# Turning the second half of q of batch 0 on VectorE, with the keys laid over row groups, in a fused attention and feed-forward kernel

## The chip, the cores and the metric

One core of one Trainium2 chip. The metric is device time in microseconds (us) of one execution.

## The reference, cut to what matters

```python
# batch 8, heads 8, seq 1024, head_dim 64, k_proj 64
k_proj = einsum('ks,bhsd->bhkd', E, k);  v_proj = einsum('ks,bhsd->bhkd', F, v)
attn   = softmax(q @ k_proj^T / 8)                   # 64 keys for each query
x      = (attn @ v_proj), heads side by side         # 8192 x 512
h      = max(x @ w1, x @ w2, x @ w3)                 # 512 -> 768
out    = h @ w_out                                   # 768 -> 512
```

## The kernel before: the parts concerned

The matmuls of the scores take q with the head dimension on the partitions (`qT`). For later batches VectorE turns q (`q_flip`, 0.69 us for each 128x512), and the kernel reads the result as 32x32 blocks, each turned in its place; the scores run as 32-row matmuls on eight tiles of the array (L141: 32 of 256 columns take 0.59 us from the first start to the next L208, though each is 0.27 us long). The second half of q of batch 0 is turned by TensorE in the kernel before:

```python
def q_up0():
    for g in range(NPAIR):
        for sl in range(4):
            for u in range(2):                      # 32 matmuls against the identity
                nc.tensor.matmul(out=ps[u*D:(u+1)*D, 4+g, sl*P:(sl+1)*P],
                                 lhsT=q_1[:, HEAD[2*g+u], sl, :], rhs=ident, start=True, stop=True)
    for j in range(2):                              # two casts out of PSUM, one on each engine
        (nc.vector.tensor_copy if j else nc.scalar.copy)(out=qT[0][...], in_=ps[...])

def scores_up0():
    for g, bank in ((0, 4), (1, 5), (2, 6), (3, 7)):
        scores0(1, g, bank)                         # 2 matmuls of 64 rows x 512 columns
    for g in (0, 2):
        nc.scalar.activation(out=pT[0][:, g:g+2, 1, :], in_=ps[:, 4+g:6+g, :], func=AF.Exp, scale=scale)
```

Loads go out from GpSimd in one order: k and v of batch 0, w1, w2, first half of w3, **second half of q of batch 0**, **second half of w3**, w_out, then k, v and q of batch 1. `kv(b)` projects keys and values of batch b, and sends the keys through a transposing DMA (`kpT`); `scores(b, u)` waits for that DMA. What each batch does is placed by slots; a slot is one 128x512 product of the feed-forward (four or six matmuls). In the first 18 us TensorE also runs `warmup` matmuls on zeros while it waits for loads. `sums` adds up the denominators of the softmax, and AV is the product of the attention weights with the projected values. `ps` is the tile in PSUM that every matmul writes: eight banks of 512 columns.

```python
if b == 0:
    at(9, scores_up0); at(12, sums0, 1, 4); at(19, kv, 1)
    # q_flip(1, g) at 21, 22, 24, 25; load_behind_turn(2) at 22
    at(27, scores, 1, 0); at(30, scores, 1, 1); at(33, sums, 1)
    # ... cut
elif b == 1:
    at(2, kv, 2)
    # ... cut
    at(9, load_behind_turn, 3, "kvq"); at(8, scores, 2, 0); at(12, scores, 2, 1)
    at(15, av1, 1); at(15, sums, 2); at(15, log, 1); at(16, recip, 0); at(18, recip, 1)
```

The softmax here doesn't subtract the row's maximum and nothing guards it: scores larger than these inputs give would overflow.

## Time and profile before

| | before |
|---|---|
| median of the first 3 runs | 396.2 us (395.97 to 396.36) |
| span of the profiled run | 394.4 us |
| TensorE busy | 98% |
| TensorE waits between 45 and 92 us of the span | 0.7 us for the turned keys of batch 2 |

The lines of the profile are in the prediction.

### The profile page before, as it was taken

Reading aid. Unit: us, or ns where it says so; the run is one execution under the profiler, and the core shown is the slowest. Engines: PE = TensorE matmul, PEld = TensorE weight load, DVE = VectorE, ACT = ScalarE, POOL = GpSimd, SP = SyncE. Lnnn points to the kernel's source line nnn. Section 1 sums busy time; section 2 is a strip of 40 time slices with the busy share of each in tenths; the row PEclk is TensorE's granted clock in tenths of the full one; section 3 lists DMA queues with packets and bytes.
Section 4 is the critical chain, followed back from the end, with each engine's and each line's share of the span. In section 5 each row is a group of like instructions: output and inputs, shape, how many; then the busy total and the mean of one; then the engine's idle time right before and its main releaser. Section 6 shows DMA issues by size and latency. Waiting matters only on the chain.

```text
span 394.4 us, 6594 instructions
## 1 busy us (share of the span) xinstructions
PE 384.6 (98%) x2691; PEld 173.5 (44%) x2742; DVE 201.0 (51%) x296; ACT 162.5 (41%) x247; POOL 66.5 (17%) x109
## 2 busy tenths in 40 slices
PE   8999999999999999999999999999999999999996
PEld 4444444444444444444444444444444444444443
DVE  3347475655653476435763357525664456443342
ACT  4414447364326622455224732266234552222221
POOL 7442141062003401050000500000010000000000
PEclk9999999999999999999999999999999999999999
DMA  8999979979953995169611892121011111101023
GB/s 223 206 209 206 206 182 199 224 118 205 206 144 83 186 206 183 26 122 202 173 53 28 166 207 108 55 74 61 2 53 55 53 56 53 56 39 67 2 106 106
DMA packets 41437, 48.39 MB, mean 123 GB/s; under 512 B 9152, under 2 KB 36544, under 8 KB 41408
## 3 DMA queue, kind: packets, MB, share of 16 engines
q0 software_dynamic: 31776, 43.52, 53.2%
q1 hardware_dynamic: 8656, 3.41, 5.0%
q10 hardware_dynamic: 976, 1.05, 0.8%
q8 instruction: 21, 0.34, 0.3%
q14 instruction: 8, 0.07, 0.1%
HBM read 57.15 MB, written 16.78 MB: 187 GB/s over the span
## 4 chain that ended last, share of the span: by engine, by line
PE 91%; DMA 6%; issue 1%; POOL 0%; ACT 0%; DVE 0%; POOLq 0%
PE ps L208 58%; PE ps L233 19%; PE ps L119 3%; PE ps L155 3%; PE ps L431 3%; DMA w_sb<-in_moe_w_dram 2%; PE ps L141 2%; DMA k_t<-in_k_dram 2%; DMA kpT<-kp 1%; PE ps L246 1%; PE ps L422 1%; PE ps L226 1%; PE ps L264 0%; PE ps L311 0%; POOL k_t L347 0%
## 5 line engine op out<-in xcount | busy, mean ns | idle before, releaser
L208 PE MATMUL ps<-xT,w_sb 128*128 128x512 bf16 x1049 | 242.9, 379 | 1.7
L208 PEld LDWEIGHTS <-w_sb 128*128 128x128 bf16 x1080 | 103.6, 98 | 130.0 <-issue 8.6
L213 DVE TENSOR_TENSOR m<-ps,h1s 128x512 f32<-128x512 f32 x90 | 62.2, 691 | 132.4 <-PE ps L208 99.1
L233 PE MATMUL ps<-wo_sb,hT 128*128 128x512 bf16 x335 | 82.3, 379 | 0.5 <-issue 0.2
L211 ACT COPY h1s<-ps 128x512 f32<-128x512 f32 x90 | 53.0, 589 | 67.4 <-PE ps L208 67.0
L235 ACT COPY o_acc<-ps 128x512 f32<-128x512 f32 x58 | 34.0, 587 | 101.3 <-PE ps L233 85.8
L215 DVE TENSOR_TENSOR hT<-ps,m 128x512 bf16<-128x512 f32 x90 | 62.0, 689 | 10.2 <-PE ps L208 2.4
L240 POOL DMA_DIRECT2D out_dram<-o_acc x28 | 15.2, 543 | 263.2 <-ACT o_acc L235 261.1
L233 PEld LDWEIGHTS <-hT 128*128 128x128 bf16 x348 | 33.5, 98 | 41.4 <-issue 1.9
L173 DVE TENSOR_TENSOR xT<-ps,rinv 128x1024 bf16<-128x1024 f32 x28 | 33.5, 1218 | 8.8 <-PE ps L155 6.8
L146 ACT ACTIVATE pT<-ps 128x1024 bf16<-128x1024 f32 x28 | 27.1, 1021 | 7.3 <-PE ps L141 7.0
L101 DVE STREAM_TRANSPOSE qT<-q_t 128x512 f32<-128x512 f32 x28 | 18.6, 689 | 0.0
L87 POOL DMA_DIRECT2D v_t<-in_v_dram x21 | 15.3, 747 | 10.8 <-PE ps L208 4.2
L164 ACT ACTIVATE lns<-ps 128x1024 f32<-128x1024 f32 x14 | 13.6, 1021 | 5.8 <-PE ps L155 5.8
L167 ACT ACTIVATE rinv<-lns 128x1024 f32<-128x1024 f32 x14 | 14.7, 1062 | 0.0
L119 PE MATMUL ps<-k_t,eT 128*64 128x512 bf16 x56 | 13.4, 382 | 0.0
L121 PE MATMUL ps<-v_t,fT 128*64 128x512 bf16 x56 | 13.4, 381 | 0.0
L125 ACT CAST kp<-ps 64x512 bf16<-64x512 f32 x7 | 4.1, 579 | 18.5 <-PE ps L121 18.5
L87 POOL DMA_DIRECT2D k_t<-in_k_dram x14 | 10.6, 770 | 2.4 <-ACT o_acc L469 1.1
L87 POOL DMA_DIRECT2D q_t<-in_q_dram x14 | 10.6, 773 | 2.1 <-DMA wo_sb<-in_moe_w_out_dram 1.1
L431 PE MATMUL ps<-xT,w_sb 128*128 128x512 bf16 x46 | 10.6, 379 | 0.2 <-issue 0.2
L127 DVE COPY kp<-kp 64x1536 bf16<-64x1536 bf16 x7 | 3.9, 552 | 12.4 <-ACT kp L125 12.4
(84 smaller groups left out, 163.3 us busy)
## 6 DMA issues: line engine op xcount, KB each, us to landing
out_dram<-o_acc POOLq DMA_DIRECT2D x30, 512.0 KB, 3.1
q_t<-in_q_dram POOLq DMA_DIRECT2D x15, 512.0 KB, 12.1
k_t<-in_k_dram POOLq DMA_DIRECT2D x14, 512.0 KB, 12.6
v_t<-in_v_dram POOLq DMA_DIRECT2D x18, 256.0 KB, 14.8
v_t<-in_v_dram POOLq DMA_DIRECT2D x7, 512.0 KB, 14.8
w_sb<-in_moe_w_dram POOLq DMA_DIRECT2D x4, 384.0 KB, 10.1
k_t<-in_k_dram POOLq DMA_DIRECT2D x4, 256.0 KB, 8.0
w_sb<-in_moe_w_dram POOLq DMA_DIRECT2D x4, 192.0 KB, 9.6
```

The lines of the kernel that those rows point to most:

```text
L87: nc.gpsimd.dma_start(out=dst[b % NB][:, slots], in_=sv[:, heads])
L101: nc.vector.transpose(out=qT[b % NB][:, hs].bitcast(FP32).rearrange("p h n -> p (h n)"), in_=q_t[b % NB][:, hs].rearrange("p h si d -> p ( ...
L119: nc.tensor.matmul(out=ps[0:KP, bank, :], lhsT=eT[:, si, :], rhs=k_t[i][:, :, si, :], start=(si == 0), stop=(si == SI - 1))
L146: nc.scalar.activation(out=pT[i][:, 2 * u + gg].rearrange("p ch (t r n) -> p r (ch t) n", t=4, r=4), in_=ps[:, AB:AB + 4, gg * 256:(gg + 1 ...
L173: nc.vector.tensor_tensor(out=xT[b % 2][:, f::2, ch, :], in0=ps[:, bank:bank + 2, :], in1=rinv[ch].rearrange("p (u n) -> p u n", u=2), op= ...
L208: nc.tensor.matmul(out=ps[:, bank, :], lhsT=w_sb[i][:, ct, jt * P:(jt + 1) * P], rhs=xT[b % 2][:, ct, ch, :], start=(ct == 0), stop=(ct == ...
L211: nc.scalar.copy(out=h1s[jt % 2], in_=ps[:, bank, :])
L213: nc.vector.tensor_tensor(out=m12[jt % 2], in0=ps[:, bank, :], in1=h1s[jt % 2], op=ALU.max)
L215: nc.vector.tensor_tensor(out=hT[c % 2][:, jt, :], in0=ps[:, bank, :], in1=m12[jt % 2], op=ALU.max)
L233: nc.tensor.matmul(out=ps[:, bank, :], lhsT=hT[c % 2][:, jt, tt * P:(tt + 1) * P], rhs=wo_sb[:, jt, :], start=(jt == 0), stop=(jt == NJT - 1))
L235: nc.scalar.copy(out=o[:, tt, :], in_=ps[:, bank, :])
L431: nc.tensor.matmul(out=ps[:, bank, :], lhsT=w_sb[i][:, ct, jt * P:(jt + 1) * P], rhs=xT[0][:, ct, 0, :], start=(ct == 0), stop=(ct == NCT ...
```

## The change

The intent: spare TensorE 32 transposes. VectorE turns this half of q in one instruction (128x1024). The changed kernel reads its result as 32x32 blocks too, each turned in its place. With such blocks the scores run on 32-row groups, and the keys of batch 0 lie on all four of them; four matmuls with a selecting matrix do that early on, in the place of two warming matmuls. Besides, AV and sums of batch 2 move one slot.

```diff
+    def kp_up0():
+        for u in range(2):
+            for f in range(2):
+                nc.tensor.matmul(out=ps[:, u, f*256:(f+1)*256], lhsT=sel[:, 2*u+f, :], rhs=kpT[0][:, 0:NPAIR, 0, :], ...)
+            nc.vector.tensor_copy(out=kp_0[:, u]..., in_=ps[:, u, :])
     def q_up0():
-        # 32 matmuls, two casts
+        nc.vector.transpose(out=qT_1 as fp32, in_=q_1 as fp32)        # 128x1024
     def scores_up0():
-        # 8 matmuls of 64 rows x 512 columns, two exps
+        # for g, f, r, u: 64 matmuls of 32 rows x 128 columns on 4 row groups x 2 column groups
+        # four exps
@@ start
+    # sel: four VectorE copies from the identity
-    warmup(1, 2)
+    kp_up0()
     sums_part0(1)
-    warmup(4, 2)
+    warmup(3, 2)
@@ b == 1
-            at(8, scores, 2, 0)
+            at(9, scores, 2, 0)
-            at(15, av1, 1)  # and sums, log at 15, recip at 16 and 18
+            at(16, av1, 1)  # and sums, log at 16, recip at 17 and 19
```

More of the change, by code (lines that the diff above doesn't have):

```diff
@@ L40 @@
     warm = T([P, 512], BF16, "warm")
+    sel = T([P, 4, P], BF16, "sel")
+    kp_0 = T([P, 2, 2, NPAIR, KP], BF16, "kp_0")
     eT = T([P, SI, KP], BF16, "eT")
@@ L304, in norm0 @@
                                     in1=rinv[ch][:, hh * 512:(hh + 1) * 512], op=ALU.mult)
+    def kp_up0():
+        for u in range(2):
+            for f in range(2):
+                nc.tensor.matmul(out=ps[:, u, f * 256:(f + 1) * 256], lhsT=sel[:, 2 * u + f, :],
+                                 rhs=kpT[0][:, 0:NPAIR, 0, :], start=True, stop=True)
+            nc.vector.tensor_copy(out=kp_0[:, u].rearrange("p f g k -> p (f g k)"), in_=ps[:, u, :])
+    qT_1 = qT[0][:, 4:8].rearrange("p a n -> p (a n)").rearrange("p (h n) -> p h n", h=H)
@@ L307, in q_up0, with scores_up0 @@
     def q_up0():
+        nc.vector.transpose(out=qT_1.bitcast(FP32).rearrange("p h n -> p (h n)"),
+                            in_=q_1.rearrange("p h n d -> p (h n d)").bitcast(FP32))
+    def scores_up0():
         for g in range(NPAIR):
-            for sl in range(4):
-                for u in range(2):
-                    nc.tensor.matmul(out=ps[u * D:(u + 1) * D, 4 + g, sl * P:(sl + 1) * P], lhsT=q_1[:, HEAD[2 * g + u], sl, :],
-                                     rhs=ident, start=True, stop=True)
@@ L313, in q_up0 @@
-        for j in range(2):
-            (nc.vector.tensor_copy if j else nc.scalar.copy)(
-                out=qT[0][:, 4 + 2 * j:6 + 2 * j].rearrange("p h n -> p (h n)"),
-                in_=ps[:, 4 + 2 * j:6 + 2 * j, :].rearrange("p b n -> p (b n)"))
-    def scores_up0():
-        for g, bank in ((0, 4), (1, 5), (2, 6), (3, 7)):
-            scores0(1, g, bank)
-        for g in (0, 2):
-            nc.scalar.activation(out=pT[0][:, g:g + 2, 1, :], in_=ps[:, 4 + g:6 + g, :], func=AF.Exp, scale=scale)
+            for f in range(2):
+                for r in range(4):
+                    rows = slice(r * HD, (r + 1) * HD)
+                    for u in range(2):
+                        nc.tensor.matmul(out=ps[half(g, u), AB + r, g * P:(g + 1) * P], lhsT=kp_0[rows, u, f, g, :],
+                                         rhs=qT_1[rows, HEAD[2 * g + u]].rearrange("p (n f) -> p n f", f=2)[:, :, f],
+                                         start=(f == 0), stop=(f == 1), tile_position=(r * HD, half(g, u).start))
@@ L324, in av_up0 @@
+        for g in range(NPAIR):
+            nc.scalar.activation(out=pT[0][:, g, 1, :].rearrange("p (n r t) -> p r n t", n=4, r=4),
+                                 in_=ps[:, AB:AB + 4, g * P:(g + 1) * P].rearrange("p r (n t) -> p r n t", n=4),
+                                 func=AF.Exp, scale=scale)
     def av_up0():
@@ L364 @@
     nc.vector.memset(ones, 1.0)
+    for u in range(2):
+        for f in range(2):
+            nc.vector.tensor_copy(out=sel[:, 2 * u + f, :].rearrange("p (r dd) -> p r dd", r=4),
+                                  in_=ident[:, None, u * D + f:(u + 1) * D:2].to_broadcast([P, 4, HD]))
     warmup(9, 7)
@@ L499 @@
             at(9, load_behind_turn, 3, "kvq")
-            at(8, scores, 2, 0)
+            at(9, scores, 2, 0)
             at(12, scores, 2, 1)
-            at(15, av1, 1)
-            at(15, sums, 2)
-            at(15, log, 1)
-            at(16, recip, 0)
-            at(18, recip, 1)
+            at(16, av1, 1)
+            at(16, sums, 2)
+            at(16, log, 1)
+            at(17, recip, 0)
+            at(19, recip, 1)
             at(24, load, 4, k, k_t)
```

## The prediction

> **What bounds the kernel now.** I read four views in this order: the page (which engine is busy), the chain that ended last (what each part waits for), the order in time of the stage that the change touches, and single DMA issues with their landings. The page first:
>
> ```profile
> PE 384.6 (98%) x2691; PEld 173.5 (44%) x2742; DVE 201.0 (51%) x296; ACT 162.5 (41%) x247; POOL 66.5 (17%) x109
> PEclk9999999999999999999999999999999999999999
> DMA  8999979979953995169611892121011111101023
> PE 91%; DMA 6%; issue 1%; POOL 0%; ACT 0%; DVE 0%; POOLq 0%
> ```
>
> Over the whole span TensorE is the bound: 98% busy at full clock, 91% of the chain. But the DMA digits are 9 in nearly all of the first five slices of 9.86 us, so the first 50 us, where the change is, can have another limit. The chain in order of time (start, length, what) says so:
>
> ```profile
> 2.32 7.76 DMA k_t<-in_k_dram
> 10.38 9.81 DMA w_sb<-in_moe_w_dram
> 20.46 0.59 PE ps L422 x2
> ...
> 31.47 0.34 PE ps L311 x8
> 31.86 0.86 PE ps L311 x24
> 32.72 1.40 PE ps L431 x6
> 34.12 0.56 PE ps L284 x8
> ...
> 74.12 5.59 DMA kpT<-kp
> 79.76 0.66 PE ps L141 x29
> ```
>
> Up to 20.2 us the chain is loads; then it is TensorE, until the transposing DMA for the keys of batch 2 holds it up at 79.76. The lines that the change replaces are L311 (the 32 transposes of q) and L284 (the 8 scores). In order of time, TensorE alone:
>
> ```profile
> 29.36 2.11 PE L431 MATMUL ps<-xT,w_sb 128*128 128x512 bf16 x8
> 31.40 1.32 PE L311 MATMUL ps<-ident,q_t 128*64 128x128 bf16 x32
> 32.65 1.47 PE L431 MATMUL ps<-xT,w_sb 128*128 128x512 bf16 x6
> 34.05 0.63 PE L284 MATMUL ps<-qT,kpT 64*64 64x512 bf16 x8
> 34.83 0.38 PE L431 MATMUL ps<-xT,w_sb 128*128 128x512 bf16 x1 [0.16 <-issue]
> ```
>
> No data wait is seen here. What must be asked is which loads landed shortly before TensorE used them, for an earlier TensorE meets those. I looked at two: the second half of w3, which the L431 group at 32.65 reads first, and the last part of v of batch 1, which the projection at L121 reads first. The first was issued at 19.54, the second at 30.82:
>
> ```profile
> L362 POOL DMA_DIRECT2D w_sb<-in_moe_w_dram x1: 542/542/542, 19.5 to 19.5; - x1
> DMA to landing us min/median/max: 12.6/12.6/12.6
> ```
> ```profile
> L87 POOL DMA_DIRECT2D v_t<-in_v_dram x1: 716/716/716, 30.8 to 30.8; - x1
> DMA to landing us min/median/max: 15.3/15.3/15.3
> ```
> ```profile
> 46.18 0.40 PE L119 MATMUL ps<-k_t,eT 128*64 128x512 bf16 x1
> 46.24 0.38 PE L121 MATMUL ps<-v_t,fT 128*64 128x512 bf16 x1
> ```
>
> 19.54 + 12.6 = 32.1 to 32.2: the w3 half lands 0.5 us before use. 30.82 + 15.3 = 46.1 to 46.2: v of batch 1 lands as L121 starts (46.24). This is the line on which my prediction hangs: the projection of batch 1 cannot start earlier unless that load lands earlier.
>
> [...] (1) [...] in the stretch from 20 to 60 us the engines are full to about 54 us at some 200 GB/s, and issue to landing takes 12 to 16 us, so several loads are always in the queue[...]. (2) [...] eight L431 matmuls from 29.36 at 0.216 us end their turn at 31.09, but L311 starts at 31.40: 0.3 us lost. (3) [...] small matmuls on different row and column groups run at once. The trace agrees: 32 matmuls of 256 columns (L141) take 0.59 us from 55.07 to the next L208 at 55.66, though each is 0.27 us long. (4) [...] its cost I take from the trace (L101, 128x512 f32, 689 ns).
>
> **The change part by part.**
> Removed: 32 transposes. L431 could follow at 31.09 in place of 32.65: 1.56 us of TensorE. Also a ScalarE cast of 1.01 us and a VectorE cast of 1.23 us (L314).
>
> Added on VectorE: one transpose of 8 x 256 bf16 seen as 128x1024 f32. 512 elements take 0.69 us and 1024 elements of other operations 1.22 us, so an estimate is 1.22 us, just that of the cast it replaces. It does not wait for TensorE; it waits for q (issued 18.21, landed by 30.3) and the six L434 operations before it, which end at 31.80. So it ends near 33.0, where the cast ended at 33.99.
>
> Added at the start: four copies that build the selector, while VectorE waits 3.2 us for E: hidden. Four selecting matmuls of 256 columns, 4 x 0.11 = 0.44 us, in place of two warming ones of 512, 2 x 0.216 = 0.43 us: no change. Two VectorE evictions of 128x512, 2 x 0.65 = 1.3 us, from about 15.0; VectorE was idle from 15.03 to 16.79: hidden. That stage ends on w1 anyway (landing at 20.2).
>
> Scores: 64 matmuls of 128 columns in place of 8 of 512. On eight tiles that is 8 rounds x 0.054 = 0.43 us, plus 0.16 us of drain (what L141 has over its own 4 x 0.107): 0.59 us if the array is the limit. Pairs of load and matmul have not started closer than 12.6 ns apart with 64-column weights (L141: (0.66 - 0.27)/31), which gives 64 x 12.6 ns + 0.16 = 0.97 us. I take 0.6 to 1.2, centre 0.9, against 0.78 (34.05 to 34.83). ScalarE exps: four of 0.6 us after the last of these matmuls, some 2.1 to 2.4 us in place of 1.94, ending near 37 at the latest while the sums need them at about 37.2: nearly hidden.
>
> The path: TensorE reaches the second w3 half at 31.1 and waits for 32.19; with 0.1 to 0.2 us to get going it starts near 32.3 to 32.45, 0.2 to 0.35 us sooner than 32.65. So of 1.56 us only some 0.3 is left. The six matmuls end at about 33.7, after the VectorE transpose (33.0), so scores do not wait for it. Minus 0.1 us for dearer scores: about 0.2 us early. From there to 46 everything is TensorE, so it arrives at the projection 0.2 us early and waits 0.2 us for v of batch 1. L121 starts at 46.24 as before. What is left: 0.0 us.
>
> Later: the words say scores of batch 2 a step later, but the order of instructions does not move them: they already stood behind a load listed for slot 9. What moves is AV and sums of batch 2 (24 matmuls) behind four L208 matmuls. At 86.33 TensorE went into them without a data wait, so I give this 0.0, within 0.2 us. The wait for the transposing DMA before 79.76 (0.75 us on TensorE) hangs on the key chain and DMA queue after 46 us, and stays.
>
> Sum: 396.2 - 0.0, and a tenth for luck with landings: 396.1 us.
>
> **The rivals.** A, TensorE is the bound everywhere: 1.56 us removed, scores about equal, so 394.6 to 394.9. For it: 98% busy, 91% of the chain, and no data wait in the stage. Against it: both landings above. I give it 1 in 10, mostly for loads that land sooner in a shifted program. B, the loads take it all (mine): 395.8 to 396.4. C, scores turn out issue-bound: at the 35 ns of L311 ((1.32 - 0.22)/31) 64 cost 2.3 us, 1.5 us more than before, and TensorE arrives at the projection over 1 us late: 397.4. Against it: that pace is of full-height weights[...]. I give it 1 in 8; half-way cases make 396.5. D, the exps, now four and after a later last matmul, stall the sums: at most 0.3 us.
>
> **Range and chances.** Three runs before span 0.4 us. B and its noise give 395.8 to 396.4; part of A and of C widen it to 395.3 to 396.9. Two per cent is 7.9 us, five times all that was removed: within 2% at 0.98, faster 0.01, slower 0.01.
>
> **What would show it.** Right: a new TensorE wait of about 1 us on w_sb before the second half of that L431 group, near 31.2 to 32.2; a wait on v_t of 0.1 to 0.4 us at the projection; L121 starting within 0.2 us of 46.24; the transpose at about 1.2 us on VectorE ending near 33.0; scores of 0.6 to 1.2 us; scores of batch 2 starting near 79.8 still after a DMA wait. Wrong: v of batch 1 landing near 45 (then A), the projection starting after 46.5 with no DMA wait (then C), or the wait at 79.76 gone or doubled.

The sum came to 396.1 us: 396.2 of before, 0.0 for the change, and a tenth for luck. "Its cost" under (4) is that of a transpose on VectorE. The 0.054 and 0.107 us for 128 and 256 columns are estimates, a quarter and about a half of the 0.216 us from start to start of the 512-column L431 matmuls; "drain" is only a name for what L141's 0.59 us have over 4 x 0.107. The 12.6 ns are L141's average, not a least: in the packed records its first eight matmuls start within 23 ns. The 0.1 to 0.2 us "to get going" are the author's estimate, without a source. In the profile after, it is 0.04 us at the second half of w3 (landed 32.52, first use 32.56) and 0.10 at v.

## The result, and the profile after

| | before | after |
|---|---|---|
| median of 6 fast runs each, same rounds | 396.09 us (395.52 to 396.8) | 397.56 us (397.45 to 398.27) |
| ratio, 95% interval | | 1.0039 (1.0026 to 1.0052) |
| span of the profiled run | 394.4 us | 395.7 us |

A ratio is the mean time of one kernel's fast runs over the mean of the other's fast runs of the same rounds, so it is not quite the ratio of the medians. A thousandth is 0.4 us here. The change makes the kernel 1.5 us slower. That is within 2% of before, but outside the predicted range of 395.3 to 396.9.

First the page of the changed kernel: less TensorE busy, more of the chain on DMA (6% before).

```profile
PE 383.8 (97%) x2717; PEld 173.4 (44%) x2768; DVE 202.8 (51%) x302; ACT 161.8 (41%) x248; POOL 66.4 (17%) x109
...
PE 88%; DMA 9%; issue 1%; ACT 0%; DVE 0%; POOL 0%; POOLq 0%; DVEq 0%
```

So the work did fall, and waiting rose by more. Where? TensorE in order of time, in the stage of the change and at the projection of batch 1 (start, length, what; in brackets the idle time before and what ended it):

```profile
29.71 2.10 PE L448 MATMUL ps<-xT,w_sb 128*128 128x512 bf16 x8
32.56 1.47 PE L448 MATMUL ps<-xT,w_sb 128*128 128x512 bf16 x6 [0.75 <-DMA w_sb<-in_moe_w_dram]
33.96 0.76 PE L329 MATMUL ps<-qT,kp 32*64 32x128 bf16 x64
34.88 2.54 PE L448 MATMUL ps<-xT,w_sb 128*128 128x512 bf16 x11 [0.16 <-issue]
...
46.23 0.40 PE L121 MATMUL ps<-k_t,eT 128*64 128x512 bf16 x1
46.62 0.38 PE L123 MATMUL ps<-v_t,fT 128*64 128x512 bf16 x1
```

The second half of w3 holds TensorE at 32.56, and v of batch 1 holds the first value matmul until 46.62, 0.39 us after the key matmul that started at 46.23. In the packed records of this profile that load landed at 46.52; before it was 46.15. From the landing to the start of the value matmul it is 0.10 us here, where TensorE waited for it, and it was 0.09 before: v had no slack in the kernel before either.

Next, TensorE's waits from 45 to 92 us, of the kernel before and then of the changed one (who, for what: total, times, longest):

```profile
PE ps L141 <- DMA kpT<-kp: 0.7, 1, 0.7
```
```profile
PE ps L143 <- DMA kpT<-kp: 1.1, 1, 1.1
PE ps L157 <- DVE hT L217: 0.5, 1, 0.5
```

The wait for `kpT` looks like the same wait grown by 0.4, but it is another one. The places in order of time show that:

```profile
56.57 0.66 PE L143 MATMUL ps<-qT,kpT 32*64 32x256 bf16 x32 [1.05 <-DMA kpT<-kp]
...
80.44 0.66 PE L143 MATMUL ps<-qT,kpT 32*64 32x256 bf16 x32
...
88.45 0.41 PE L157 MATMUL ps<-pT,vp 64*32 64x512 bf16 x8 [0.50 <-DVE hT L217]
```

The wait before (79.76) was for the keys of batch 2. It is gone, and the keys of batch 1 are awaited instead, at 56.57. With the starts of the same pieces of work in both traces, the account of the lateness is:

| TensorE starts | before | after | later by |
|---|---|---|---|
| values of batch 1 | 46.24 | 46.62 | 0.38 |
| scores of batch 1 | 55.07 | 56.57 | 1.50 |
| projection of batch 2 | 70.95 | 72.45 | 1.50 |
| scores of batch 2 | 79.76 | 80.44 | 0.68 |
| next w_out group behind AV of batch 2 | 92.35 | 93.55 | 1.20 |
| end of the span | 394.4 | 395.7 | 1.3 |

Three losses (0.38 at the values, 1.12 at the scores of batch 1, 0.52 at AV), and one gain of 0.82: the scores of batch 2 wait no more. TensorE's lateness alone does not explain this gain, as the DMA for the keys of batch 2 was issued 1.50 us later too (75.62 against 74.12). That DMA took 4.6 us from issue to landing where it took 5.6 (landed at 80.24 and at 79.72). Why it was shorter is not shown.

**Why do the keys of batch 1 come late?** The DMA queues in the window from 52.2 to 55 us, in which these keys are moved; before, then after (queue: packets, MB, time of the packets as a share of 16 engines):

```profile
q1 hardware_dynamic: 1054, 0.26, 61.2%
q0 software_dynamic: 69, 0.22, 19.5%
```
```profile
q1 hardware_dynamic: 734, 0.19, 131.5%
q0 software_dynamic: 76, 0.24, 20.9%
q8 instruction: 1, 0.02, 4.9%
```

q1 is the transposing DMA. The stores on q0 are the same. But its packets take more than twice the engine time, fewer of them are done, and an instruction fetch (q8) stands in the window. From issue to landing the DMA takes 6.8 us against 5.5. (The time of the packets is no sure sign: in the same window it is 76.2% in e1 below, where the DMA took 6.9 us, and 87.0% in e4, where it took 5.5.) By the pages of both profiles, q8 moves 0.34 MB in 21 packets, 16 KB each; the page of before lists 5,433 TensorE instructions (2,691 matmuls, 2,742 weight loads). Counted in the packed records of before, TensorE starts 166 to 341 matmuls and weight loads from one fetch to the next, 247 on average; some records can be missing. I take q8 to be TensorE's fetches, as the fetch of this place moves when nothing but TensorE's instructions is added (56.0 in before, 52.84 in e3, 51.33 in e7, both below); that is inferred. The changed kernel has 52 more TensorE instructions ahead of this point (+8 selecting, -4 warming, -64 and -16 removed, +128 added), and its fetch starts at 52.66 where it started at 56.0 before.

### The profile page after: what moved, and what is told of

Its sections match the earlier page's. It is cut to its first block, busy times and chain, and to the rows that moved or that the text cites. A ratio compares the mean times of both kernels' runs of the same rounds, so it can differ in the third digit from the quotient of the medians.

```text
span 395.7 us, 6653 instructions
## 1 busy us (share of the span) xinstructions
PE 383.8 (97%) x2717; PEld 173.4 (44%) x2768; DVE 202.8 (51%) x302; ACT 161.8 (41%) x248; POOL 66.4 (17%) x109
## 4 chain that ended last, share of the span: by engine, by line
PE 88%; DMA 9%; issue 1%; ACT 0%; DVE 0%; POOL 0%; POOLq 0%; DVEq 0%
PE ps L210 57%; PE ps L235 19%; DMA w_sb<-in_moe_w_dram 3%; PE ps L121 3%; PE ps L157 3%; DMA v_t<-in_v_dram 3%; PE ps L143 2%; DMA k_t<-in_k_dram 2%; DMA kpT<-kp 2%; PE ps L248 1%; PE ps L448 1%; PE ps L228 1%; PE ps L123 0%; PE ps L266 0%; DVE hT L217 0%
## 5 line engine op out<-in xcount | busy, mean ns | idle before, releaser
L89 POOL DMA_DIRECT2D v_t<-in_v_dram x21 | 15.3, 751 | 10.3 <-DMA q_t<-in_q_dram 3.9
L121 PE MATMUL ps<-k_t,eT 128*64 128x512 bf16 x56 | 13.6, 382 | 0.0
L448 PE MATMUL ps<-xT,w_sb 128*128 128x512 bf16 x46 | 10.6, 379 | 1.0 <-DMA w_sb<-in_moe_w_dram 0.8
```

The source lines that it names most:

```text
L89: nc.gpsimd.dma_start(out=dst[b % NB][:, slots], in_=sv[:, heads])
L121: nc.tensor.matmul(out=ps[0:KP, bank, :], lhsT=eT[:, si, :], rhs=k_t[i][:, :, si, :], start=(si == 0), stop=(si == SI - 1))
```

## The experiments

Theory: there are two losses. (1) The 52 extra instructions move a fetch into the transposing DMA. (2) The moved AV of batch 2 waits for a bank of PSUM. Rivals: the changed work is dear in itself (more scores, later exps); the lateness is chance; the slot only shows lateness from elsewhere. All ten kernels gave correct results. Each was timed in five rounds. The kernel before had medians of 395.75 us beside e1 to e4, 396.07 beside e5 to e8, and 396.29 beside e9 and e10, so ratios are compared.

Instructions were added without adding work: a warming matmul of 512 columns was cut in two or four, in a stage that waits for loads.

```diff
-    def warmup(n, bank):
-        for _ in range(n):  # 512 columns
+    def warmup(n, bank, cut=1):
+        for _ in range(n * cut):  # 512 // cut columns
```

**e1: the changed kernel with the old slots for AV and sums of batch 2.**

```diff
-            at(16, av1, 1); at(16, sums, 2); at(16, log, 1); at(17, recip, 0); at(19, recip, 1)
+            at(15, av1, 1); at(15, sums, 2); at(15, log, 1); at(16, recip, 0); at(18, recip, 1)
```

> The changed kernel with AV and sums of batch 2 back in their old slot. Theory (two losses, one of them the slot): the new stall of 0.5 us on VectorE's eviction ahead of that AV goes, so the time falls by 0.5 to 0.6 us against the changed kernel, to about +0.9 us over before. Rival (the slot only takes up slack left by lateness elsewhere): the stall turns up again within the next 10 us and the time stays at +1.4.

396.93 us, ratio 1.003 (1.0018 to 1.0042), so +1.2 us. The stall at AV is gone and did not come back: one wait above 0.2 us is left between 45 and 92 us.

```profile
PE ps L143 <- DMA kpT<-kp: 1.2, 1, 1.2
```

The gain over the changed kernel is 0.3 to 0.4 us by the two ratios (1.0039 and 1.003, each with its own runs of before), a little under what was expected.

**e2: the kernel before with the new slots only** (the edit of e1 backwards).

> The kernel before with nothing but AV and sums of batch 2 a slot later. Theory: the stall on the eviction is a matter of which banks the pair takes, so it appears here too: +0.5 to +0.6 us over before. Rival (it appears only with the shifted timing of the changed kernel): within 0.2 us of before.

396.69 us, ratio 1.002 (1.0008 to 1.0032), +0.8 us, with the same stall:

```profile
PE ps L141 <- DMA kpT<-kp: 0.7, 1, 0.7
PE ps L155 <- DVE hT L215: 0.5, 1, 0.5
```

The slot costs time in the kernel before too. Why, can be read in the changed kernel's order of time:

```profile
84.46 1.94 ACT L148 ACTIVATE pT<-ps 128x1024 bf16<-128x1024 f32 x2 [0.87 <-PE ps L143]
...
86.28 0.59 ACT L213 COPY h1s<-ps 128x512 f32<-128x512 f32 x1
...
86.91 0.69 DVE L215 TENSOR_TENSOR m<-ps,h1s 128x512 f32<-128x512 f32 x1 [1.80 <-ACT h1s L213]
87.71 0.69 DVE L217 TENSOR_TENSOR hT<-ps,m 128x512 bf16<-128x512 f32 x1
```

Two exps hold ScalarE for 1.94 us; the copy `h1s` stands behind them, the maximum waits for the copy and `hT` for the maximum. AV takes two neighbouring banks of a ring of four. Following the kernel's own ring code with both slots, the old slot takes the pair (0, 1), and the new one the pair (2, 3); bank 2 is the one which `hT` has to empty first. So the four matmuls put ahead gave TensorE nothing to win, and the choice of banks a wait.

**e3: the kernel before with 52 more instructions** (warm-ups cut; nothing else).

```diff
-    warmup(9, 7)        # also warmup(4, 3), warmup(4, 2) and one warmup(1, 2)
+    warmup(9, 7, 2)     # and warmup(4, 3, 2), warmup(4, 2, 4), warmup(1, 2, 2): 26 matmuls more
```

> The kernel before with 52 more TensorE instructions (warming matmuls cut in two or four of the same total length) in the first 16 us, which wait for loads anyway. Theory (the row count moves an instruction fetch into the transposing DMA of batch 1): the fetch seen at 56.0 in before moves to 52 to 54, that DMA lands 1 us or more later than 54.8, TensorE waits for it about 1 us at the scores of batch 1, and of this 0.2 to 0.5 us is left at the end. Rival (the late landing comes from the changed work or from chance): the DMA lands near 54.8 and the time is that of before within 0.2 us.

396.91 us, ratio 1.0029 (1.0017 to 1.0041), +1.15 us, more than expected. The fetch starts at 52.84, the DMA lands 6.8 us after issue (56.49), and the queues from 52.2 to 55 us look as in the changed kernel:

```profile
q1 hardware_dynamic: 876, 0.22, 134.2%
q0 software_dynamic: 76, 0.23, 20.6%
q8 instruction: 1, 0.02, 4.8%
```

TensorE's waits for `kpT` are 1.9 us, in two: 1.14 at batch 1 and, unlike the changed kernel, still 0.79 at batch 2, whose keys landed at 81.23 here (80.24 in the changed kernel). The DMA for batch 2 was issued when it was in the changed kernel (75.59 against 75.62) and took 5.6 us, not 4.6. This is why more of it is left than expected in this profile, which is of the slowest of the five runs (397.69 us). No work of the change is in this kernel. The count of instructions alone makes up the first loss.

**e4: the changed kernel with 30 more instructions** (so 82 more than before; the slots stay new).

```diff
-    warmup(4, 3)        # also warmup(3, 2) and two warmup(1, 2)
+    warmup(4, 3, 2)     # and warmup(3, 2, 4), twice warmup(1, 2, 2): 15 matmuls more
```

> The changed kernel with 30 more TensorE instructions in the same stage. Theory: the fetch moves from 52.7 to about 49 to 50, before the transposing DMA moves data, so that DMA lands near 55.2 instead of 56.5, the wait of 1.05 us at the scores of batch 1 nearly goes, and the time falls by 0.2 to 0.6 us against the changed kernel (most is given back in the wait at 80 us). Rival: the DMA lands at 56 or later whatever the row count.

396.36 us, ratio 1.0014 (1.0002 to 1.0026), +0.55 us: 1 us better than the changed kernel, more than expected. The fetch starts at 50.44, before the DMA's packets (52.35), and the DMA takes 5.5 us. The wait at the scores of batch 1 is gone, and none came at batch 2 (keys landed at 78.67). The stall at AV stays:

```profile
PE ps L157 <- DVE hT L217: 0.5, 1, 0.5
PE ps L123 <- issue: 0.5, 1, 0.5
```

The second line is the wait for v of batch 1, put down to "issue": the value matmul started at 46.83, and the load had landed at 46.74.

**e5: both taken back** (e4 with the old slots).

> Both losses taken back in the changed kernel: 30 more TensorE instructions early and AV of batch 2 in its old slot. If the two losses are all and add up, the stall of 0.5 us that e4 still had at 87.5 goes and the time is that of before within 0.3 us (e4 stood at +0.55). If something of the change itself costs time too, +0.5 us or more is left.

395.87 us, ratio 1.0002 (0.999 to 1.0015): level with before. The two losses are all of the slowdown, within 0.6 us, and within the same 0.6 us the part of the change that was meant costs nothing and gives nothing.

**e7: the kernel before with 82 more instructions** (as e3, more cuts).

```diff
-    warmup(9, 7)        # also warmup(4, 2) and two warmup(1, 2)
+    warmup(9, 7, 4)     # and warmup(4, 2, 4), twice warmup(1, 2, 2): 41 matmuls more
```

> The kernel before with 82 more TensorE instructions early, as many in all as e4 and e5 have. Theory (what counts is where the fetch falls, not the cut warming matmuls): the fetch falls near 50, the transposing DMA of batch 1 lands at or before 55.5, no wait of 1 us at its scores, and the time is within 0.3 us of before or up to 0.7 us below it, if the wait at 79.8 goes as it did in e4; in any case 0.8 us or more below e3. Rival (more or cut instructions cost by themselves): as slow as e3, +1.1 us.

396.09 us, ratio 1.0 (0.9987 to 1.0013). Thirty instructions more than e3 and 1.1 us faster: more or cut instructions do not cost by themselves. It is also the control for e5, which has as many instructions and the change besides: 396.09 us here and 395.87 in e5, timed beside the same runs of before (ratios 1.0 and 1.0002), so no gain of the change stands clear of the noise. The fetch starts at 51.33 for 0.97 us and is over when the DMA's packets start (52.56); the DMA takes 5.3 us. Over all twelve profiles the DMA for the keys of batch 1 took 4.1 to 5.5 us where no fetch ran inside its packets (in e5 the two met for less than 0.1 us), and 6.8 to 6.9 us in the three where one did (after, e1, e3). Both waits for keys are gone in this profile. That its span (395.1 us) is not below before's has to do with v of batch 1, which landed at 47.06. But it is the profile of the slowest of the five runs (396.94 us), as that of e5 is of the slowest of its six (396.76), so neither shows the median run.

The same traces hold a cleaner comparison: the key DMAs of batches 4 to 7, with no packet of another queue beside theirs but the fetches. In e4, for batch 5 (165.5 to 171 us) and then for batch 6 (212 to 217.5 us):

```profile
q8 instruction: 1, 0.02, 1.1%
kpT<-kp SPq DMA_TRANSPOSE x1, 4.7
```
```profile
kpT<-kp SPq DMA_TRANSPOSE x1, 3.5
```

Over the twelve profiles, 34 of these 48 DMAs have no fetch inside their packets and take 3.46 to 3.60 us. The other 14 (batches 5 and 7 of e4 to e10) have one of 0.89 to 1.24 us and take 4.46 to 4.73 us. Batches 4 and 6 of the same seven kernels are among the 34. In the 14, all but 28 to 99 of the 1056 packets start within 1.92 us of the first, the time in which all of them are done without a fetch; the rest come later. A fetch inside the packets thus costs this DMA about 1 us, with nothing else in play. A long time alone does not tell of a fetch: among loads and stores the key DMA of batch 3 took 5.7 to 7.3 us in the twelve profiles, in none of them with a fetch inside its packets.

**e6 and e8: the projection and scores of batch 1 one slot later,** in e5 and in e7.

```diff
-            at(19, kv, 1);  at(27, scores, 1, 0);  at(30, scores, 1, 1)
+            at(20, kv, 1);  at(28, scores, 1, 0);  at(31, scores, 1, 1)
```

> As e5, with the projection of batch 1 and its scores one slot (four matmuls, 0.86 us) later, so that TensorE has other work until v of batch 1 lands. Theory (v of batch 1 holds what the removed transposes saved): the wait at the projection of some 0.3 to 0.5 us goes and the time falls by 0.3 to 0.5 us under e5, below before. Rival (the saving is used up before the projection, or the lateness of the keys comes back at the scores): within 0.2 us of e5.

> As e7 with the projection and scores of batch 1 one slot later, as e6 has: a control for e6. Theory: TensorE of the kernel before reaches the projection only as v lands, so the slot gives nothing here: within 0.2 us of e7. Rival (the slot itself is what helps in e6): 0.3 us or more below e7.

e6: 395.88 us, ratio 0.9999 (0.9987 to 1.0011), no better than e5. e8: 396.58 us, ratio 1.0016 (1.0004 to 1.0028), 0.6 us worse than e7, where no effect was expected. What the theory expected missed in both, for one reason, here in e6:

```profile
62.24 0.62 PE L157 MATMUL ps<-pT,ones 64*32 64x512 bf16 x16 [0.46 <-ACT pT L148]
```

The projection no longer waited (values at 47.37, landing 46.78), but with the scores later and the sums in place, the sums waited 0.46 us for the exps, and as long in e8. In e8, without the saving, it is a plain loss.

**e9: e6 with the sums of batch 1 one slot later too.**

```diff
-            at(33, sums, 1); at(33, log, 1); at(34, recip, 0)
+            at(34, sums, 1); at(34, log, 1); at(35, recip, 0)
```

> As e6, with the sums of batch 1 one slot later too. In e6 the sums waited 0.46 us for the exps of batch 1. Theory (the saving was turned into that wait): the wait goes and the time falls by 0.3 to 0.5 us under e6, 0.1 to 0.5 us below before. Rival (another chain, such as the landing of the keys of batch 2, takes it again): within 0.2 us of before.

395.44 us against 396.29, ratio 0.9984 (0.9967 to 1.0), -0.6 us; span 393.6. TensorE has no wait left between 45 and 92 us. The interval just reaches 1.0.

**e10: e9 with the second half of w3 loaded before the second half of q.** In the kernel before, q had to come first, because TensorE turned it ahead of the w3 group.

```diff
     for hh in range(2):
-        if wt is w_sb[2] and hh: dma_start(out=q_1, in_=qv_[1])
         dma_start(out=wt[...], in_=w[...])
+    dma_start(out=q_1, in_=qv_[1])
```

> As e9, with the second half of w3 loaded ahead of the second half of q. Theory (the second half of w3 held 1.2 of the 1.56 us that the removed transposes left free): it lands near 30 instead of 32.3, the wait on w_sb of 0.7 us goes, the scores start some 0.4 us sooner (when the later q is turned) and the time falls by up to another 0.5 us, if nothing behind takes it. Rival (the projection of batch 1 then waits for v again): the wait turns up there and the time stays within 0.2 us of e9.

395.49 us, ratio 0.998 (0.9965 to 0.9994). Against e9 nothing, so the expected gain failed to come. The w3 half landed at 29.67 and TensorE did not wait for it, but q landed at 32.39, VectorE turned it then, and the scores start where they started in e9 (33.71):

```profile
33.71 0.76 PE L329 MATMUL ps<-qT,kp 32*64 32x128 bf16 x64 [0.73 <-DVE qT L320]
```

Two loads in one queue stand before the scores, and swapping them swaps the name of the wait, not its end. e9 and e10 are the fastest versions found, by 0.2% of the kernel before. No run has their slots and added instructions without the change (e8 has the sums in the old slot), so how much of this comes from the change is not shown.

## Why the prediction was wrong, point by point

**Right, and shown:** the bound of this stage. TensorE reached the second half of w3 early, waited for it (0.75 us) and started 0.09 us sooner than before; with the scores, which took 0.92 us from start to the next L448 (predicted 0.9, before 0.78), all that was saved was spent by 34.88, where it was 34.83 before. The 0.09 us is less than the predicted 0.2 to 0.35, as the load landed at 32.52 and not at 32.19. The transpose on VectorE took 1.23 us (predicted 1.22) and the scores did not wait for it. The exps, 2.06 us, held up nothing. At the projection TensorE waited for v of batch 1, as predicted.

**Right by luck, or misread on the way:** the 0.9 us for the scores. The matmuls started 8.5 ns apart on average, closer than the 12.6 ns that the sum took as the least, while 0.38 us passed from the last start to the next L448, where the sum had 0.16. The two errors cancel. Also, a record is missing among the eight L431 matmuls: the starts in the packed records run from 29.36 to 31.09 at 0.216 us, with a gap of two steps at 30.23, so their turn ends at 31.31. Then 0.09 us were lost before L311, where the shape of the tiles changes, and not the 0.3 that the prediction read; what costs them is not shown. The transposes removed were worth 1.34 us, not 1.56. The "12 to 16 us" from issue to landing are medians of groups; the three parts of v of batch 1 took 15.3 to 17.5.

**Wrong, step one: "L121 starts at 46.24 as before. What is left: 0.0 us."** The values started 0.38 us later, as v landed 0.37 us later. I treated a landing as fixed, and v had no slack to take up a later one. e4, e5, e6 and e9 have the same instructions up to these loads, and v landed at 46.74, 47.56, 46.78 and 46.31. The first load of k landed at 9.07, 10.05, 9.69 and 8.99 in them, so much of this scatter is there from the start; that the change itself makes v later is not shown. The prediction thought of the spread of landings as "a tenth for luck" and, in rival A, of loads that land sooner; it left out one that lands later.

**Wrong, step two: that after the projection the one wait on keys is that before 79.76, which "hangs on the key chain and DMA queue after 46 us, and stays".** No new wait was expected between 46 and 79.76. None lay at the scores of batch 1 before, but I did not ask by how little: the keys landed at 54.81 in the packed records and the scores started at 55.07. The transposing DMA took 1.3 us longer, because of 52 instructions which I had counted as matmul time only. e3 shows it without the change, e4 and e7 that it goes when the fetch falls elsewhere. And the wait at 79.76, which I said stays, was gone (one of the prediction's own signs of being wrong) and gave back 0.82 us, as the DMA for the keys of batch 2 took 1.0 us less. This is the term that cost most: 1.1 us at its place; +1.15 us in e3 by itself.

**Wrong, step three: "I give this 0.0, within 0.2 us" for the moved AV.** It cost 0.52 us in the trace, and +0.8 us by itself in e2. I looked whether TensorE waited for data there, not which banks the moved instruction would take. The remark that the scores of batch 2 do not move held: the order of instructions moved AV and sums alone.

**Rival C came near the number (397.4) for a wrong reason.** Its pace of 35 ns for each score matmul would have made 2.3 us; they took 0.92. Its sign, a late projection with no DMA wait, did not appear. A forecast that fits the time is not thereby right.

**Open.** How one fetch on q8 holds back the DMA is not shown; the records do not say which of the 16 engines a packet ran on. That it is the fetch rests on its place in twelve profiles, on two counts of instructions, and on the key DMAs of batches 4 to 7, where nothing else differs that the records show. That q8 is TensorE's is inferred. Why e5 and e7, without any of the key waits, are level with before and not 0.7 us below it is not settled either: in both profiles, each of the slowest run of its kernel, v of batch 1 landed about 1 us later than in the profile of before. There is no profile of a median run of them, nor one of before from the same chip.

## What to carry to other kernels

Here time taken off TensorE counted only up to the next load that it met (of 1.34 us, 0.09 were left at the second half of w3), so list for each such load its landing beside its first use, and write down the slack: v had none (0.09 us from landing to use, as where TensorE waits for it), and the keys landed 0.26 us before their use, which was used up here. A change of the number of TensorE instructions moved an instruction fetch too (52 more, from 56.0 to 52.84 us, in e3); when a DMA far from the change is suddenly slow, add or cut instructions that cost nothing and look whether it moves. When two small edits come together, undo each alone: here the rider (one slot) cost 0.8 us by itself (e2), and the main part won nothing that stands clear of the noise (e5 beside e7).
